# Sink rows of v by their own small transfers, and joint sink scores, in a windowed-attention kernel with a channel-mix FFN

## The chip, the cores and the metric

The kernel runs on one core of one Trainium2 chip. The metric is device time in microseconds for one execution, the median of several runs. A core has five engines that run side by side and wait for one another by semaphores: PE (matrix products), DVE (vector work), ACT (activations and copies), POOL (general work) and SP (which here issues transfers). SBUF is the on-chip memory, PSUM the eight banks into which PE writes.

## The reference

Attention with a window of 128 keys and 4 sink keys that every query sees, and on its output an FFN with a token shift:

```
q, k, v: (4, 8, 768, 64) float32      # batch, heads, positions, head width
scores = q @ k^T / sqrt(64)
keep   = (key position < 4) | (0 <= query position - key position < 128)
a      = softmax(where(keep, scores, -1e9));   attn = a @ v
x      = attn as (4, 768, 512);  x_prev = x shifted by one position
xk     = mu_k * x + (1 - mu_k) * x_prev;  xr = mu_r * x + (1 - mu_r) * x_prev
out    = sigmoid(xr @ w_r) * (relu(xk @ w_k)^2 @ w_v)      # 512 -> 1024 -> 512
```

## The kernel before

The work is cut into 12 units of 256 positions, three to each of the four sequences (u = 3b + T, with T = 0, 1, 2). A unit passes these steps, each a function that files its operations with a planner (`Plan.op`):

- `load` fetches q, k, v by transfers on SP's queue; two 1 MB halves of `w_k` and `w_v` and the whole of `w_r` come between the first units.
- `prepare` casts q and k to bf16 (`qb`, `kb`), transposes them on PE through a bank, or by a transposing transfer from a later unit on, and copies the bank to `qt` and `kt`; v is cast to `vb`, which has a column of ones beside each head's 64 values, so that a product gives the softmax sum as well.
- `attend` makes the scores of two head pairs at a time (`sc`), their exponentials on ACT (`e`), the mask as a product on DVE, and the products with the values (`o`, a bank for each head pair). DVE then takes the reciprocal of the sums (`rec`) and scales into `x`.
- `mix` transposes x into `xt` (on PE, or by transfers) and makes on DVE the difference to the previous position (`td`) and from it `xk` and `xr`.
- `ffn` does for the unit before: four groups of products with `w_k` (`kp` in the planner's keys, line L1139), relu (`rl`) on ACT and square (`kk`) on DVE, the gate's products (`rp`, L1170) with a tanh (`th`), and the products with `w_v` (`vp`, L1188 and, for the last block, L1108), which DVE joins with the gate into `ob` (L1197) for the store.

The sinks: in units with T = 1 or 2, the four sink keys lie outside the window for most queries. `sink_keys` places the four keys of each head from `kt` of the sequence's first unit into a small stationary matrix `ksink`. `sink_scores` (L835) makes for a unit the scores of all heads against the sinks, four products of 256 columns into one bank, and ACT makes their exponentials `es` (L842). For the values, once in each sequence, PE multiplies the whole first half of `vb` (128 rows of 512 columns) with a 0/1 matrix `spread` (L814), which puts the four sink rows of v onto the partitions where the sink scores of each head lie, and DVE multiplies the bank with a head mask `hmask` into `vsink` (L818, two buffers). `sink_values` (L924, or L909 in another tiling) adds the sinks' part to `o`.

Nothing is ordered at run time. `ORDER` lists for each engine the numbers of its operations, in the order in which it takes them, and `CHOICE` says for some operations which engine does them (or how PE is tiled). `Plan.schedule` walks these lists, hands out buffers and banks, and puts warm-up products on `warm` (L1251, L1254, L1248) where its own clock has PE waiting in the first 28 us. An engine waits at an operation until its inputs are there, and all that stands behind it in its list waits too. The numbers change whenever an operation is added or removed, so the two kernels' lists are not comparable by number; what follows therefore names operations by what they write.

Four pools matter around the change: two double banks for the scores, four single banks for everything else that PE writes, three buffers `ob`, and five `e`.

Of the kernel before, what the change touches and what calls it, by code (L numbers as in the profile page):

```python
# [8 lines left out]
FP32 = mybir.dt.float32  # L9
# [9 lines left out]
    80: "ACT", 81: "POOL", 82: "ACT", 83: "DVE", 84: "POOL", 85: "ACT", 86: "ACT",  # L19
    87: "ACT", 88: "ACT", 89: "DVE", 90: "DVE", 92: "ACT", 93: "ACT", 95: "ACT", 96:  # L20
    "POOL", 98: "ACT", 99: "DVE", 101: "DVE", 102: "POOL", 103: "ACT", 129: "POOL",
    131: "ACT", 132: "DVE", 134: "ACT", 135: "ACT", 137: "ACT", 138: "DVE", 140:
    "ACT", 141: "POOL", 142: "DVE", 144: "DVE", 151: "ACT", 160: "PE/tiles", 172:
    "PE/tiles", 183: "POOL", 185: "ACT", 186: "ACT", 188: "ACT", 189: "POOL", 191:
    "ACT", 192: "POOL", 194: "ACT", 195: "DVE", 196: "DVE", 198: "DVE", 205: "ACT",
    213: "ACT", 217: "ACT", 221: "ACT", 225: "ACT", 234: "SP", 238: "POOL", 242:
    "PE/full", 254: "PE/tiles", 265: "POOL", 267: "ACT", 268: "DVE", 270: "ACT",
    271: "POOL", 273: "DVE", 274: "DVE", 276: "ACT", 277: "POOL", 278: "ACT", 283:
    "DVE", 290: "DVE", 298: "ACT", 302: "ACT", 306: "ACT", 310: "ACT", 319: "SP",
    323: "SP", 346: "ACT", 348: "ACT", 349: "DVE", 351: "ACT", 352: "ACT", 354:  # L30
    "ACT", 355: "ACT", 357: "ACT", 358: "POOL", 359: "POOL", 361: "ACT", 368: "ACT",
    376: "ACT", 380: "ACT", 384: "ACT", 388: "ACT", 397: "SP", 401: "SP", 405:
    "PE/tiles", 417: "PE/tiles", 428: "POOL", 429: "POOL", 431: "ACT", 432: "POOL",
    434: "POOL", 436: "ACT", 437: "POOL", 438: "ACT", 440: "ACT", 447: "ACT", 455:
    "ACT", 459: "ACT", 463: "ACT", 467: "ACT", 476: "SP", 480: "SP", 484:
    "PE/tiles", 496: "PE/tiles", 507: "POOL", 508: "ACT", 510: "ACT", 511: "POOL",
    513: "ACT", 515: "ACT", 516: "ACT", 517: "ACT", 522: "ACT", 529: "ACT", 537:
# [38 lines left out]
TOGETHER = 2  # L76

OCT = range(1, 12)

WHOLE = (0,)  # L80

JOINT = ()

SWITCH = 95.0

LOADS = ("kq0", "v0", "kq1", "wka", "wkb", "v1", "wr", "wva", "wvb")
# [300 lines left out]
def kernel(  # L389
# [190 lines left out]
    def fill_later():  # L580
        for t in ksink + vsink:
            nc.vector.memset(t, 0.0)
# [729 lines left out]
```

## Time and profile before

| | |
|---|---|
| median of three runs | 163.79 us (162.93 to 163.96) |
| the profiled execution | 163.9 us, its span 162.2 us |
| busy PE, DVE, ACT, POOL | 152.7, 147.4, 119.9, 39.3 us |
| granted TensorE clock | 1.00 |
| moved by transfers | 35.16 MB |

In the profile, L12 means line 12 of the kernel, PEld is PE's weight load, and SPq or ACTq an engine's issuing of transfers. A name such as `kt` stands for all its buffers. A row of the chain or of the timeline begins with its start and length in us; in brackets stands how long the engine had been idle before it, and what released it. In the stretches, the columns behind the length are the busy time of PE, PEld, DVE, ACT and POOL with the instructions started, then the granted clock, the share of the transfer engines and GB/s. Busy time of PE overlaps from product to product, so 5 of 5 us does not mean that no product waited.

### The profile page before, as it was taken

The numbers are of one execution on the slowest core, as the hardware profiler recorded it, in microseconds if no ns is written. First come the engines' busy times: TensorE is split into PE (matmuls) and PEld (weight loads), VectorE is DVE, ScalarE is ACT, GpSimd is POOL, SyncE is SP. The second block draws the span as 40 slices with busy tenths as digits, with TensorE's granted clock in tenths as the row PEclk, the third lists the DMA queues.
The fourth block names the chain that finished last, engine by engine and source line by source line (L and its number), as shares of the span: only waits on it lengthen the run. The fifth ranks groups of instructions, "written<-read, shape, count | busy, mean of one in ns | idle before, by whom it ended". The sixth has DMA issues, their size and how long they took to land.

```text
span 162.2 us, 4697 instructions
## 1 busy us (share of the span) xinstructions
PE 152.7 (94%) x1857; PEld 99.4 (61%) x1857; DVE 147.4 (91%) x378; ACT 119.9 (74%) x194; POOL 39.3 (24%) x69
## 2 busy tenths in 40 slices
PE   7959779999999999999999999999999999999992
PEld 2545457964568567776566575865466865577541
DVE  6299989999999999999999999999999999998631
ACT  4699998999999899888689964878167985043420
POOL 6643330610662260242111006241010040001000
PEclk9999999999999999999999999999999999999999
DMA  4999999999988999999999999999999733351113
GB/s 140 251 353 249 391 342 295 368 401 312 211 265 215 259 233 156 237 266 144 223 213 211 303 220 207 196 265 164 265 168 206 168 89 103 65 195 68 65 65 129
DMA packets 78885, 35.16 MB, mean 217 GB/s; under 512 B 68744, under 2 KB 71056, under 8 KB 78864
## 3 DMA queue, kind: packets, MB, share of 16 engines
q1 hardware_dynamic: 78384, 33.63, 88.7%
q0 software_dynamic: 320, 1.05, 1.8%
q8 instruction: 14, 0.23, 0.7%
q10 hardware_dynamic: 160, 0.20, 0.3%
q14 instruction: 7, 0.06, 0.1%
HBM read 24.12 MB, written 6.29 MB: 188 GB/s over the span
## 4 chain that ended last, share of the span: by engine, by line
PE 75%; DVE 7%; SPq 5%; DMA 5%; ACT 3%; issue 2%; POOL 1%; DVEq 0%
PE bank L1188 24%; PE bank L1139 22%; PE bank L1170 12%; PE bank L971 6%; DMA ks<-in_k_dram 5%; PE sc L866 5%; SPq L483 2%; DVE e L952 2%; SPq L500 2%; ACT rl L1149 2%; PE bank L1012 2%; PE bank L754 1%; PE bank L924 1%; SPq L507 1%; DVE x L988 1%
## 5 line engine op out<-in xcount | busy, mean ns | idle before, releaser
L1139 PE MATMUL bank<-xk,wk_sb 128*128 128x256 bf16 x384 | 48.3, 273 | 0.0
L938 ACT ACTIVATE e<-sc 128x1024 bf16<-128x1024 f32 (+1 forms) x48 | 45.0, 965 | 2.3 <-PE sc L866 2.1
L1188 PE MATMUL bank<-wv_h,kk 128*128 128x512 bf16 x184 | 44.8, 379 | 0.0
L1139 PEld LDWEIGHTS <-wk_sb 128*128 128x128 bf16 x384 | 36.0, 98 | 7.2
L1149 ACT ACTIVATE rl<-bank 128x512 bf16<-128x512 f32 x47 | 27.2, 608 | 15.6 <-PE bank L1139 13.8
L952 DVE TENSOR_TENSOR e<-e,mask 128x1024 bf16<-128x1024 bf16 (+1 forms) x48 | 31.0, 659 | 0.0
L1188 PEld LDWEIGHTS <-kk 128*128 128x128 bf16 x184 | 17.0, 98 | 15.8
L1061 DVE SCALAR_TENSOR_TENSOR xr<-td,mu_all,xt 128x256 bf16<-128x256 bf16 x48 | 24.0, 514 | 0.0
L1170 PE MATMUL bank<-wr_sb,xr 128*128 128x512 bf16 x96 | 23.7, 379 | 0.4 <-DVE vsink L818 0.4
L1061 DVE SCALAR_TENSOR_TENSOR xk<-td,mu_all,xt 128x256 bf16<-128x256 bf16 x48 | 23.9, 526 | 0.1
L1161 DVE TENSOR_TENSOR kk<-rl 128x512 bf16<-128x512 bf16 x48 | 20.9, 451 | 1.8 <-ACT rl L1149 1.7
L1176 ACT ACTIVATE th<-bank 128x512 f32<-128x512 f32 x24 | 14.1, 598 | 10.9 <-PE bank L1170 10.9
L988 DVE TENSOR_TENSOR x<-bank,rec 128x256 bf16<-128x256 f32 x48 | 19.4, 416 | 0.3
L1197 DVE SCALAR_TENSOR_TENSOR ob<-th,bank 128x512 f32<-128x512 f32 x23 | 15.5, 679 | 2.7 <-ACT th L1176 2.5
L971 PE MATMUL bank<-vb,e 128*128 128x65 bf16 x352 | 16.4, 194 | 1.3 <-DVE e L952 1.2
L791 POOL CAST vb<-vs 128x512 bf16<-128x512 f32 x10 | 9.4, 948 | 31.8 <-DMA vs<-in_v_dram 22.1
L971 PEld LDWEIGHTS <-e 128*128 128x128 bf16 x352 | 13.8, 97 | 5.4 <-DVE e L952 2.5
L1170 PEld LDWEIGHTS <-xr 128*128 128x128 bf16 x96 | 8.8, 98 | 9.3 <-issue 0.5
L866 PEld LDWEIGHTS <-kt 64*64 64x64 bf16 (+1 forms) x496 | 8.9, 106 | 6.4 <-issue 3.8
L866 PE MATMUL sc<-qt,kt 64*64 64x128 bf16 (+4 forms) x496 | 12.6, 226 | 0.0
L1048 DVE TENSOR_TENSOR td<-xt 128x512 bf16<-128x512 bf16 x24 | 10.6, 455 | 0.0
L714 POOL CAST qb<-qs 128x512 bf16<-128x512 f32 x7 | 5.1, 722 | 21.8 <-DMA qs<-in_q_dram 21.8
(95 smaller groups left out, 150.9 us busy)
## 6 DMA issues: line engine op xcount, KB each, us to landing
vs<-in_v_dram SPq DMA_DIRECT2D x24, 256.0 KB, 5.0
out_dram<-ob SPq DMA_DIRECT2D x19, 256.0 KB, 3.9
ks<-in_k_dram SPq DMA_DIRECT2D x16, 256.0 KB, 5.1
qs<-in_q_dram SPq DMA_DIRECT2D x12, 256.0 KB, 4.0
qs<-in_q_dram SPq DMA_DIRECT2D x6, 512.0 KB, 5.8
ks<-in_k_dram SPq DMA_DIRECT2D x4, 512.0 KB, 8.4
w<-in_moe_w_k_dram SPq DMA_DIRECT2D x2, 1024.0 KB, 8.8
w<-in_moe_w_v_dram SPq DMA_DIRECT2D x2, 1024.0 KB, 10.4
```

The lines of the kernel that those rows point to most:

```text
L866: nc.tensor.matmul(out=sc[keys, a, o0 + f0 - q0:o0 + f1 - q0], lhsT=lhs[rows, keys], rhs=qs[rows, f0:f1], start=u not in BIAS, stop=True, ...
L938: nc.scalar.activation(out=buf[ek][:, :, lo:], in_=buf[sck][:, :, lo:], func=AF.Exp, scale=scale)
L952: nc.vector.tensor_tensor(out=at, in0=at, in1=m, op=ALU.mult)
L971: nc.tensor.matmul(out=o[:, g, a, :], lhsT=e[:, a, e0:e0 + 128], rhs=rhs, start=(T == 0 and i == 0), stop=(i == len(blocks) - 1), skip_gro ...
L988: P.op("DVE", dve(256), lambda ok=ok, rk=rk, c=c: nc.vector.tensor_tensor(out=buf["x", u][:, :, 128 * c:128 * c + 128].rearrange("p g (a d ...
L1061: nc.vector.scalar_tensor_tensor(out=buf[key][:, c, :], in0=buf[tk][:, i, :], scalar=mu[w][:, c:c + 1], in1=xt[:, c, t0 - 1:t0 + 255], op0 ...
L1139: nc.tensor.matmul(out=ps[:, i, :], lhsT=wk_sb[:, c, 128 * f:128 * f + 128], rhs=xk[:, c, :], start=(c == 0), stop=(c == NC - 1), skip_gro ...
L1149: nc.scalar.activation(out=buf[rk], in_=buf[psk].rearrange("p (i t) -> p i t", i=2), func=AF.Relu)
L1161: P.op("DVE", dve(512, 0.52), lambda f2=f2, rk=rk: nc.vector.tensor_tensor(out=buf["kk", u][:, 2 * f2:2 * f2 + 2, :], in0=buf[rk], in1=buf ...
L1170: nc.tensor.matmul(out=buf[psk], lhsT=buf["xr", u][:, c, 128 * g:128 * g + 128], rhs=wr_sb[:, c, :], start=(c == 0), stop=(c == NC - 1))
L1188: nc.tensor.matmul(out=buf[psk], rhs=wv_h[:, f, :], lhsT=buf["kk", u][:, f, 128 * g:128 * g + 128], start=(f == 0), stop=(f == NF - 1))
L1197: P.op("DVE", dve(512), lambda psk=psk, tk=tk, bk=bk: nc.vector.scalar_tensor_tensor(out=buf[bk], in0=buf[tk], scalar=1.0, in1=buf[psk], o ...
```

## The change

The sink rows of v no longer come from `vb` of each sequence's first unit. Four transfers on ACT's queue, of 32 rows of 64 floats each, fetch them for all sequences and heads at the start (`vs32`), an engine casts them (`vs16`, here DVE), four products of 64 columns with a wider `spread` (a matrix for each sequence) put them in one bank, ACT copies the bank to `rows` (with a column of ones), and DVE makes `vsink` for each sequence from `rows` and `hmask`, both bf16 in SBUF; `vsink` has four buffers now and is no longer cleared. `spread` is made by eight small copies on POOL in place of two, ahead of the mask of the first units; POOL's `make_sinks` goes. In sequences 1, 2 and 3 (`JOINT`) the sink scores of T = 1 and T = 2 are made together, eight products in one bank, with one exponential of 512 columns; `prepare` of the third unit is filed ahead of `attend` of the second. All of `ORDER` and `CHOICE` is new.

```diff
-JOINT = ()
+JOINT = (1, 2, 3)
...
 ORDER = {
     "PE": (
-        94, 91, 107, 78, 97, 100, 105, 118, 110, 115, 130, 136, 143, 133, 121, 139,
+        101, 81, 98, 112, 104, 77, 107, 123, 115, 120, 148, 141, 135, 126, 138, 144,
...
-    spread = tile1([128, 128], BF16, "spread")
+    spread = tile1([128, B, 128], BF16, "spread")
+    vs32 = tile1([128, D], FP32, "vs32")
+    vs16 = tile1([128, D], BF16, "vs16")
+    rows = tile1([128, B, D + 1], BF16, "rows")
...
-    vsink = [tile1([128, H, D + 1], BF16, f"vsink{i}") for i in range(2)]
+    vsink = [tile1([128, H, D + 1], BF16, f"vsink{i}") for i in range(B)]
...
-        for t, value in ((ones, 1.0), (spread, 0.0), (hmask, 1.0)):
+        for t, value in ((ones, 1.0), (spread, 0.0), (hmask, 1.0), (rows, 1.0)):
...
-        for t in ksink + vsink:
+        for t in ksink:
...
     def make_spread():
-
+        to = spread.rearrange("p b (k i w) -> p b i k w", k=2, i=2)
+        at = ident.rearrange("p (s b i k a) -> p a s b i k", s=NS, b=B, i=2, k=2)
         for a in range(2):
-            nc.gpsimd.tensor_copy(
-                out=spread[0:NS, :].rearrange("p (c w) -> p c w", w=32)[:, :, 4 * a:4 * a + NS],
-                in_=ident[0:NS, 0:NS].unsqueeze(1).to_broadcast([NS, NP, NS]))
+            for j in range(NS):
+                nc.gpsimd.tensor_copy(out=to[:, :, :, :, NS * a + j], in_=at[:, a, j])
...
-    def make_sinks():
-        for t in vsink:
-            nc.gpsimd.tensor_copy(out=t[:, :, D:D + 1], in_=hmask[:, :, D:D + 1])
...
+    def load_sinks():
+        for j in range(NS):
+            nc.scalar.dma_start(out=vs32[B * H * j:B * H * j + B * H, :],
+                                in_=v[:, :, j, :].rearrange("b h d -> (b h) d"))
+    P.op("ACT", 1200.0, load_sinks, -98, writes=["vs32"], service=90.0, descs=128, lag=2500.0)
...
+    def spread_sinks():
+        for b in range(B):
+            nc.tensor.matmul(out=buf["vsp"][:, D * b:D * b + D], lhsT=spread[:, b, :], rhs=vs16,
+                             start=True, stop=True)
+    P.op("PE", 150.0, spread_sinks, -38, take=[("bank", "vsp")], reads=["spread", "vs16"],
+        writes=["vsp"])
...
+    for b in range(B):
+        P.op("DVE", dve(520, 0.52), lambda b=b: nc.vector.tensor_tensor(
+            out=vsink[b], in0=rows[:, b, :].unsqueeze(1).to_broadcast([128, H, D + 1]),
+            in1=hmask, op=ALU.mult), 30 * b - 30, port=True, reads=["rows", "hmask"],
+            writes=[("vsink", b)])
...
-        psk = ("vsp", b)
-        P.op("PE", 220.0, lambda: nc.tensor.matmul(
-            out=buf[psk].rearrange("p (h d) -> p h d", h=H), lhsT=spread,
-            rhs=buf["vb", u][:, 0, :, 0:D], start=True, stop=True), rank + 4,
-            take=[("bank", psk)], hold=[("vb", u)], reads=["spread", ("vb", u, 0)], writes=[psk])
-        P.op("DVE", dve(512), lambda: nc.vector.tensor_tensor(
-            out=vsink[b % 2][:, :, 0:D], op=ALU.mult, in1=hmask[:, :, 0:D],
-            in0=buf[psk].rearrange("p (h d) -> p h d", h=H)), rank + 4, hold=[psk],
-            reads=[psk, "hmask", "sinks"], writes=[("vsink", b % 2)])
```

Three places of the new order. The first is PE's list at the very start, between the first transposes of unit 0's q and those of its k. Before (the product on `warm` is a warm-up):

```order
L759 MATMUL bank_63<-ident,qb_82 128x128
L1251 LDWEIGHTS warm
L1251 MATMUL bank_64<-warm 128x512
L759 LDWEIGHTS kb_79
L759 MATMUL bank_66<-ident,kb_79 128x128
```

And now, where `vs_151` is the cast rows of the sinks (this is the last of four such products):

```order
L675 LDWEIGHTS spread
L675 MATMUL bank_64<-vs_151,spread 128x64
L785 LDWEIGHTS kb_79
L785 MATMUL bank_66<-ident,kb_79 128x128
L785 LDWEIGHTS kb_79
```

The spreading of all sequences now stands ahead of the first transposes of k; before, the first sequence's stood behind the first scores, and the others' in the later units.

The second is DVE's list after the memsets of the start, up to the first mask (`e_94`). Before:

```order
L719 CAST kb_79<-ks_67 128x4x2x64
L719 CAST qb_82<-qs_70 128x4x2x64
L777 COPY qt_89<-bank_64 128x512
L660 COPY mu_all<-bank_63 128x8
L952 TENSOR_TENSOR e_94<-e_94,mask_147 128x2x384
```

And now:

```order
L745 CAST qb_82<-qs_70 128x4x2x64
L668 CAST vs_151<-vs_150 128x64
L803 COPY qt_89<-bank_63 128x512
L803 COPY kt_85<-bank_66 128x512
L745 CAST qb_82<-qs_70 128x4x2x64
L687 TENSOR_TENSOR vsink_157<-rows,hmask 128x520
L745 CAST kb_79<-ks_67 128x4x2x64
L803 COPY kt_85<-bank_64 128x512
L967 TENSOR_TENSOR e_94<-e_94,mask_147 128x2x384
```

The cast of the sinks' rows, both copies of unit 0's kt and the second sequence's vsink now stand on DVE ahead of the first mask; the copies of kt were ACT's.

The third is DVE's list near the end, from unit 11's last mask (`e_97`) to the last piece of unit 10's xk (`xk_115`), `x_109` being unit 11's. Before:

```order
L952 TENSOR_TENSOR e_97<-e_97,mask 128x1024
L985 RECIPROCAL rec_103<-bank_66 128x4
L988 TENSOR_TENSOR x_109<-bank_66,rec_103 128x2x128
L985 RECIPROCAL rec_106<-bank_63 128x4
L985 RECIPROCAL rec_105<-bank_65 128x4
L988 TENSOR_TENSOR x_109<-bank_65,rec_105 128x2x128
L1048 TENSOR_TENSOR td_110<-xt_156 128x512
L988 TENSOR_TENSOR x_109<-bank_63,rec_106 128x2x128
L1048 TENSOR_TENSOR td_112<-xt_156 128x512
L1061 SCALAR_TENSOR_TENSOR xk_115<-td_110,mu_all,xt_156 128x256 x2
L1061 SCALAR_TENSOR_TENSOR xk_115<-td_112,mu_all,xt_156 128x256 x2
```

And now, from the same mask, without its first rows on:

```order
L1076 SCALAR_TENSOR_TENSOR xk_115<-td_111,mu_all,xt_161 128x256
L1212 SCALAR_TENSOR_TENSOR ob_132<-th_129,bank_63 128x512
L1063 TENSOR_TENSOR td_110<-xt_161 128x512
L1000 RECIPROCAL rec_105<-bank_64 128x4
L1000 RECIPROCAL rec_106<-bank_65 128x4
L1076 SCALAR_TENSOR_TENSOR xk_115<-td_110,mu_all,xt_161 128x256
L1003 TENSOR_TENSOR x_109<-bank_64,rec_105 128x2x128
L1003 TENSOR_TENSOR x_109<-bank_65,rec_106 128x2x128
L1076 SCALAR_TENSOR_TENSOR xk_115<-td_110,mu_all,xt_161 128x256
L1076 SCALAR_TENSOR_TENSOR xk_115<-td_111,mu_all,xt_161 128x256
```

An `ob` has moved into the piece and the xk are spread among unit 11's x. On PE, between unit 11's last values and the first `kp` of unit 10, five half products with `w_v` stood before and three stand now.

More of the change, by code (lines that the diff above doesn't have):

```diff
@@ L18 @@
 CHOICE = {
[L19 to L37, printed above, removed]
-    "ACT", 541: "ACT", 545: "ACT", 549: "ACT", 558: "SP", 562: "SP", 585: "ACT",
@@ L52 @@
+    "ACT", 984: "SP", 988: "SP", 991: "ACT", 995: "ACT", 999: "ACT", 1003: "DVE",
+    1012: "SP",
 }
```

79 lines of the change are left out of this document (55 added, 24 removed), and 137 rows, old and new, of the table ORDER.

## Prediction

> **What bounds the kernel now.** I read first the page's lines on busy time and the chain that ended last, then that chain in order of time, then the engines' busy time by stretches, and last the single instructions at the places that those three point to.
>
> ```profile
> PE 152.7 (94%) x1857; PEld 99.4 (61%) x1857; DVE 147.4 (91%) x378; ACT 119.9 (74%) x194; POOL 39.3 (24%) x69
> PE 75%; DVE 7%; SPq 5%; DMA 5%; ACT 3%; issue 2%; POOL 1%; DVEq 0%
> ...
> 10.17 8.74 DMA ks<-in_k_dram
> 18.97 0.82 POOL kb L710
> ...
> 110.02 0.61 DVE vsink L818
> 110.67 1.02 PE bank L1170 x4
> ...
> 8.70:24.00 15.30, 11.60 (x219) 7.52 (x219) 14.39 (x38) 14.38 (x24) 5.39 (x9) 1.00 1.07 340
> 24.00:60.00 36.00, 35.61 (x477) 23.87 (x479) 35.93 (x91) 34.78 (x56) 11.97 (x16) 1.00 1.03 283
> 60.00:100.00 40.00, 40.00 (x524) 27.07 (x517) 39.43 (x101) 33.47 (x56) 9.26 (x13) 1.00 1.18 220
> 100.00:140.60 40.60, 40.23 (x500) 25.88 (x499) 39.85 (x105) 26.30 (x42) 6.34 (x10) 1.00 0.85 174
> ```
>
> The first two lines say PE. The chain in time (start and length in us) says where it does not hold: before about 24 us the chain runs over the keys of unit 2 (the transfer lands at 18.97) and what is made of them, and at 110 it runs over DVE. The stretches (length, then busy PE, weight loads, DVE, ACT, POOL) say something that the shares hide: from 8.7 to 140.6 us DVE is busy 129.6 of 131.9 us. PE and DVE are a dead heat, and PE takes its work in a fixed order, so whichever is later at a handover sets the pace. Two handovers show it:
>
> ```profile
> 20.70 0.42 DVE L1021 COPY xt<-bank 128x512 bf16<-128x512 bf16 x1 [0.65 <-PE bank L1012]
> 23.56 0.41 PE L971 MATMUL bank<-vb,e 128*128 128x65 bf16 x8 [0.87 <-DVE e L952]
> 23.82 1.03 PE L1139 MATMUL bank<-xk,wk_sb 128*128 128x256 bf16 x8
> ...
> 135.77 0.67 DVE L952 TENSOR_TENSOR e<-e,mask 128x1024 bf16<-128x1024 bf16 x1
> 137.06 4.48 PE L1188 MATMUL bank<-wv_h,kk 128*128 128x512 bf16 x20
> 138.89 1.67 DVE L1061 SCALAR_TENSOR_TENSOR xk<-td,mu_all,xt 128x256 bf16<-128x256 bf16 x4
> 141.38 2.78 PE L1139 MATMUL bank<-xk,wk_sb 128*128 128x256 bf16 x24
> ```
>
> The FFN begins at 23.82 behind a wait for a mask. At the end DVE finishes unit 10's xk at 140.56 (138.89 + 1.67) and PE wants it at 141.38: 0.8 us to spare after 130 us. From there on the chain is PE's alone, so the time is the start of that L1139 plus a fixed tail of 22.5 us (163.9 - 141.4).
>
> **The change, part by part.** All sums are against the profiled execution, 163.9 us with a span of 162.2; the median of the runs is 163.79, 0.1 below.
>
> *PE.* Four spreading products of 512 columns go, four of 64 columns come at the very start; three of the four stood in the full stretch. In sequences 1 to 3 two sink-score operations become one of twice the length.
>
> ```profile
> 47.19 0.22 PE bank L814
> 47.41 0.22 PE bank L835 x4
> 47.63 0.46 PE sc L866 x16
> ...
> 66.97 0.24 PE bank L924 x8
> 67.21 0.33 PE sc L866 x16
> ...
> PE bank L1170 <- DVE vsink L818: 0.4, 1, 0.4
> ```
>
> A spreading product holds PE 0.22 us: 3 x 0.22 = 0.66. Four sink-score products take 0.22, and the scores behind them take 0.13 more than behind products of their own tiling (0.46 against 0.33). Eight in one go cost between 0.22 and 0.44, so each joint operation saves 0 to 0.22; I take the middle, 3 x 0.11 = 0.33, and 0.13 for one change of tiling fewer in the new order. With the wait that ends at 110.67 (the last row: 0.4 us in which PE was held because DVE had not yet read a spreading product's bank), PE is relieved by 0.66 + 0.33 + 0.13 + 0.4 = 1.5 us, bounds 1.0 to 1.8.
>
> *DVE from the first mask to unit 10's xk.* I counted both orders between these two points. Masks, reciprocals, normalisations, xk, xr, kk and td are the same in number; the rest differs by: 4 vsink products fewer of the old kind and 3 new ones; 4 q casts and 2 v casts fewer; one ob, 2 xt copies, one wk cast, one wv cast, one k cast, one relu and one copy of mu more; a qt copy in the place of a kt copy.
>
> ```profile
> L818 DVE TENSOR_TENSOR vsink<-bank,hmask 128x512 bf16<-128x512 f32 x4 | 2.7, 681 | 0.0
> L952 DVE TENSOR_TENSOR e<-e,mask 128x1024 bf16<-128x1024 bf16 x32 | 21.7, 688 | 0.0
> L1197 DVE SCALAR_TENSOR_TENSOR ob<-th,bank 128x512 f32<-128x512 f32 x23 | 15.5, 679 | 2.7 <-ACT th L1176 2.5 <-PE bank L1188 0.2
> L710 DVE CAST qb<-qs 128x512 bf16<-128x512 f32 x5 | 1.9, 421 | 0.1
> L791 DVE CAST vb<-vs 128x512 bf16<-128x512 f32 x4 | 1.7, 419 | 0.0
> L1021 DVE COPY xt<-bank 128x512 bf16<-128x512 bf16 x4 | 1.7, 414 | 0.7 <-PE bank L1012 0.7
> L677 DVE CAST wk_sb<-w 128x1024 bf16<-128x1024 f32 x1 | 0.7, 689 | 0.0
> L675 DVE TENSOR_SCALAR wv_h<-w 128x1024 bf16<-128x1024 f32 x1 | 0.7, 684 | 0.0
> ```
>
> An instruction's successor starts about 0.08 before its end, so each counts 0.08 less than its mean: 0.60 for the long ones (the relu, which reads a bank of the same size as ob's, is put with them), 0.34 for the short. The new vsink product (520 elements, all operands bf16 in SBUF) has no row. Its ends are 0.34 (half of a 1024-element mask, with the fixed part) and 0.61 (as the old one on PSUM); I take 0.34, nearest to the mask, which also reads a repeated bf16 operand. Then: -4 x 0.60 + 3 x 0.34 - 6 x 0.34 + 0.60 + 2 x 0.33 + 3 x 0.60 + 0.34 + 0.1 = +0.1 us. **DVE is given nothing back in this stretch**: what vsink frees is spent on copies and casts taken over from ACT and POOL. With the other end it would be 0.9 us more.
>
> The row fits a rule of the Trainium skill, "Vector Engine (DVE) Microarchitecture Reference", section "5.1 Performance modes": a product of two tensors does two elements a cycle only where all operands are 2-byte and step by one. Its stricter reading asks for 4-byte alignment, which the 130-byte rows here would break (the 0.61 end, 0.8 us more in the sum); the page reports that alignment made no difference, and rows of odd length neither. No run here shows an odd row yet.
>
> *The start.* Here the change costs. PE now has the spreading ahead of the first transposes of k, and it waits for the spread matrix (POOL) and for four small transfers issued by ACT and a cast of them on DVE.
>
> ```profile
> 0.81 0.56 ACTq L551 DMA_DIRECT2D ob<-in_moe_mu_r_dram  x1
> 1.47 0.26 ACTq L551 DMA_DIRECT2D ob<-in_moe_mu_k_dram  x1
> 4.42 0.18 POOL L603 CAST ident<-ident 8x8 f32<-8x8 bf16 x1
> 5.99 0.59 ACT L777 COPY kt<-bank 128x512 bf16<-128x512 bf16 x1
> 6.00 0.32 POOL L630 COPY spread<-ident 4x16 bf16<-4x16 bf16 x2
> 6.63 0.51 PE L866 MATMUL sc<-qt,kt 64*128 64x256 bf16 x8
> ...
> vs<-in_v_dram SPq DMA_DIRECT2D x24, 256.0 KB, 5.0
> out_dram<-ob SPq DMA_DIRECT2D x1, 64.0 KB, 2.0
> ```
>
> Two small copies took 0.32, so eight take 1.3; begun at 4.60 they end at 5.9. The transfers are issued behind one of mu, at 0.26 to 0.56 each: the last leaves at 2.7 to 3.9. The nearest rows for landing are 2.0 us (the smallest with a time) and 5.0 (a load in the same traffic), so they land between 4.7 and 8.9. I take the lower part, 4.7 to 5.8, since 8 KB is nearest to the 64 KB row; then spread is the later one. Spreading ends at 6.2, four transposes of k take until 6.6, the copy of kt, on DVE now, until 7.3 (0.59 on ACT, by DVE's other reads of a bank up to 0.69), scores at about 7.4 in place of 6.63: **0.8 us late**, bounds 0.3 and 3.3. ACT and DVE have little idle time behind that point to make it up (14.38 and 14.39 of 15.30 us in the first stretch), so DVE's first mask moves from 8.7, where that stretch begins, to 9.5.
>
> The Trainium skill, "DMA: Bandwidth & Descriptors", section "Rules for kernel authors", speaks against this edit: below 64 KB a transfer is mostly overhead. In its section "Anatomy of one DMA" the fixed part is about 2.0 us for transfers that GpSimd issues; by that estimate the last would land at 4.7 to 5.9, spread would still be later, and the sum would not change. It lowers the chance of the late case below.
>
> *What the start gains.*
>
> ```profile
> DVE rec L985 <- PE bank L971: 0.8, 3, 0.4
> ```
>
> In the new order the first FFN product does not stand behind DVE's copy of unit 1's xt, which made DVE wait 0.65 and PE 0.87. DVE thereby has its wait of 0.65 back, and of its three waits for PE's values (0.8 in all, the row above) I let half go, 0.4, as PE is earlier. The keys of unit 2 keep their place in the queue of loads and land at 19 as before; the FFN then starts at about 23.2, 0.6 earlier.
>
> *Other engines.* ACT has five sink exponentials for eight, and fewer casts and copies; it is busy 74%, so that is hidden. Four stores move from POOL's queue to SP's, behind loads already issued; nothing waits for a store but a buffer of three.
>
> *The sum.* DVE reaches unit 10's xk at 140.56 + 0.8 + 0.1 - 0.65 - 0.4 = 140.4. In the new order PE has only three half products (2.6 us) in place of five between unit 11's last values and unit 10's FFN, so it stands waiting there: L1139 starts at 140.5 in place of 141.4. The tail holds the same products. 163.9 - 0.9 = 163.0, on the runs' scale **162.8 us**.
>
> **The rivals.**
>
> *PE sets the pace.* If DVE is quicker than counted (less held up by POOL, a start only 0.3 late), PE's relief comes through whole: 1.5 + 0.6 from the earlier start = 2.1, that is 161.8. For it: the chain is 75% PE; ACT and DVE need not share so many handovers early. Against: the sum of DVE's work. It decides where DVE ends xk before 139.3.
>
> *The sinks' rows land late.* PE's queue is in order: while it waits for the spreading, k isn't transposed, no score is made, and ACT and DVE stand still. With a landing at 8.9, cast and spreading end at 9.4 in place of 6.2, scores at 10.6; the start is 4.0 late, 3.2 more than forecast. All of it passes to DVE's finish: 163.0 + 3.2 = 166.2; with a landing at 7.5, 164.8. It becomes slower than before from a landing of about 6.8. For it: the first units' loads move at the same time, and such loads take 5.0. Against: 2.0 us for the smallest row.
>
> *The gain is eaten.* New waits between 24 and 60 us, where three engines are full at once (35.61, 35.93 and 34.78 of 36.0), or unit 10's handover later than counted, bring it back to 163.8.
>
> **How the numbers follow.** DVE's pace 0.42 (162.2 to 163.4), PE's pace 0.30 (161 to 162.1), eaten 0.14, rows late 0.14. About 1% is what a measurement of this kernel can tell from no change, so faster means below 162.15 and slower above 165.4. All of PE's pace and a sixth of the forecast lie below: 0.37. Of the late case two thirds lie above: 0.09. The rest is 0.54. The range of 8 in 10 leaves out the lowest tenth, under 161.2, and the worse part of the late case: 161.2 to 165.0.
>
> **What would show it.** The first scores start at 7.4 and not 6.6; a wait of PE for spread, or for the cast of the rows, stands ahead of them. The new vsink product lasts 0.4 us, not 0.68. No spreading product after 10 us, and a joint sink-score group of eight in 0.33. The first L1139 at 23.2. DVE busy over 97% to 140 us, and PE idle ahead of unit 10's L1139 behind DVE's xk. Wrong would be: PE never waiting there (PE's pace), scores after 8.5 us (rows late), or DVE with idle time of several us.

## The result, and the profile after

The changed kernel takes 169.47 us (median; 169.33 to 170.75), the kernel before 163.49 in the same comparison: a ratio of 1.0385 (it is worked out from all runs and not from the two medians), 95% interval 1.0322 to 1.0448. It is 3.9% slower, where 162.8 us and a range up to 165.0 were forecast. The profiled execution took 169.39 us, its span 167.7 (before: 163.9 and 162.2). Here and below a ratio leaves out executions more than 1.5% above the fastest of their kernel, which in sinks_first are four of twelve (166.1 to 166.6 us).

The timeline of ACT's queue, DVE and PE at the start of the changed kernel (start and length in us, engine, line, operation, and in brackets the idle time ahead of it and what ended it):

```profile
1.11 0.55 ACTq L551 DMA_DIRECT2D ob<-in_moe_mu_k_dram  x1
1.70 0.79 ACTq L664 DMA_DIRECT2D vs<-in_v_dram  x2
3.84 1.31 ACTq L664 DMA_DIRECT2D vs<-in_v_dram  x2
6.29 0.27 ACTq L551 DMA_DIRECT2D ob<-in_moe_mu_r_dram  x1
...
4.83 0.58 PE L785 MATMUL bank<-ident,qb 128*128 128x128 bf16 x4 [0.35 <-POOL ident L597]
4.98 1.16 POOL L635 COPY spread<-ident 128x16 bf16<-128x16 bf16 x8
5.21 1.17 PE L1269 MATMUL bank<-warm 128*128 128x256 f32 x2
6.60 0.62 ACT L745 CAST kb<-ks 128x512 bf16<-128x512 f32 x1 [4.30 <-DMA qs<-in_q_dram]
8.85 0.46 DVE L668 CAST vs<-vs 128x64 bf16<-128x64 f32 x1 [4.58 <-DMA vs<-in_v_dram]
9.36 0.37 PE L675 MATMUL bank<-vs,spread 128*128 128x64 bf16 x4 [2.98 <-DVE vs L668]
9.54 0.61 PE L785 MATMUL bank<-ident,kb 128*128 128x128 bf16 x4
9.95 1.17 PE L1269 MATMUL bank<-warm 128*128 128x256 f32 x2
11.48 0.82 PE L881 MATMUL sc<-qt,kt 64*128 64x256 bf16 x8
```

and two rows of PE in the kernel before:

```profile
5.55 0.40 PE L759 MATMUL bank<-ident,kb 128*128 128x128 bf16 x4
5.79 0.65 PE L1254 MATMUL bank<-warm 128*128 128x256 f32 x2
```

Three things are to be seen. The third and fourth of the sinks' transfers are issued only from 3.84 on, and ACT's queue is occupied until 6.56, so ACT casts its first half of k at 6.60. The rows land at 8.85; DVE has been idle for 4.58 us by then, and PE for 2.98 when the cast is done. And what PE does behind that wait is slow: four transposes take 0.61, a pair of fp32 warm-up products 1.17 and eight scores 0.82, where in the kernel before the same rows read 0.40, 0.65 and 0.51. The rows of 4.83 and 5.21, ahead of the wait, are slow as well (0.58 and 1.17): in this execution PE had not become fast before the wait began. The first scores start at 11.48 instead of 6.63.

From the first FFN product to the end the two kernels take the same time. The first row below is the first FFN product (23.82 before), the second unit 10's (141.38 before):

```profile
29.15 1.48 PE L1154 MATMUL bank<-xk,wk_sb 128*128 128x256 bf16 x12
...
146.99 3.66 PE L1154 MATMUL bank<-xk,wk_sb 128*128 128x256 bf16 x32
```

From the one to the other are 117.84 us, 117.56 before; from unit 10's to the span's end 20.7, 20.8 before. So 5.3 of the span's 5.5 us are lost ahead of the first FFN product. The parts of the change that stand in the middle do what they should. A group of DVE's instructions (busy us, mean ns of one):

```profile
L687 DVE TENSOR_TENSOR vsink<-rows,hmask 128x520 bf16<-128x520 bf16 x4 | 1.7, 426 | 0.0
```

a piece of the chain in order of time:

```profile
61.20 0.33 PE bank L850 x8
```

and two stretches, before and, behind the dots, in the changed kernel (length, then busy PE, weight loads, DVE, ACT, POOL, clock, DMA share, GB/s):

```profile
40.00:60.00 20.00, 20.00 (x270) 12.48 (x272) 19.97 (x49) 19.29 (x33) 8.44 (x13) 1.00 1.00 230
60.00:80.00 20.00, 20.00 (x268) 14.22 (x264) 19.46 (x50) 17.01 (x30) 5.35 (x9) 1.00 1.23 212
...
40.00:60.00 20.00, 19.32 (x241) 12.07 (x240) 19.58 (x47) 18.66 (x30) 9.98 (x11) 1.00 0.77 188
60.00:80.00 20.00, 19.18 (x293) 12.96 (x292) 19.78 (x50) 16.44 (x28) 7.23 (x11) 1.00 1.21 221
```

A vsink product takes 0.43 us and a joint group of sink scores 0.33. But in the stretches PE is now idle for 0.7 and 0.8 us of 20, where it was busy throughout. From the first FFN product to unit 10's it is busy for 115.7 us instead of 116.8, in a stretch that is no shorter: the work taken off it became waiting.

### The profile page after: what moved, and what is told of

The parts are those of the page before. It is cut to its first block, busy times and chain, and to the rows that moved or that the text cites. A ratio compares the mean times of both kernels' runs of the same rounds, so it can differ in the third digit from the quotient of the medians.

```text
span 167.7 us, 4713 instructions
## 1 busy us (share of the span) xinstructions
PE 155.3 (93%) x1862; PEld 101.3 (60%) x1862; DVE 148.4 (89%) x381; ACT 118.4 (71%) x188; POOL 38.6 (23%) x70
## 4 chain that ended last, share of the span: by engine, by line
PE 72%; DVE 12%; issue 5%; ACT 4%; DMA 3%; SPq 1%; POOL 1%; DVEq 0%; POOLq 0%
PE bank L1154 23%; PE bank L1203 21%; PE bank L1185 12%; PE bank L986 6%; PE sc L881 5%; DMA vs<-in_v_dram 3%; DVE xk L1076 3%; DVE e L967 2%; ACT e L953 2%; PE bank L780 1%; PE bank L1027 1%; DVE x L1003 1%; SPq L507 1%; DVE td L1063 1%; DVE kk L1176 1%
## 5 line engine op out<-in xcount | busy, mean ns | idle before, releaser
L953 ACT ACTIVATE e<-sc 128x1024 bf16<-128x1024 f32 (+1 forms) x48 | 44.4, 961 | 6.7 <-PE sc L881 6.6
L967 DVE TENSOR_TENSOR e<-e,mask 128x1024 bf16<-128x1024 bf16 (+1 forms) x48 | 31.7, 678 | 0.5 <-ACT e L953 0.5
L1076 DVE SCALAR_TENSOR_TENSOR xr<-td,mu_all,xt 128x256 bf16<-128x256 bf16 x48 | 22.4, 484 | 0.0
L986 PE MATMUL bank<-vb,e 128*128 128x65 bf16 x352 | 15.7, 194 | 0.4 <-DVE e L967 0.2
L881 PE MATMUL sc<-qt,kt 64*64 64x128 bf16 (+4 forms) x496 | 13.1, 228 | 0.7 <-ACT kt L798 0.4
L1063 DVE TENSOR_TENSOR td<-xt 128x512 bf16<-128x512 bf16 x24 | 10.6, 457 | 0.0
L740 POOL CAST kb<-ks 128x512 bf16<-128x512 f32 x6 | 4.5, 761 | 20.9 <-DMA ks<-in_k_dram 20.8
```

The source lines that it names most:

```text
L881: nc.tensor.matmul(out=sc[keys, a, o0 + f0 - q0:o0 + f1 - q0], lhsT=lhs[rows, keys], rhs=qs[rows, f0:f1], start=u not in BIAS, stop=True, ...
L953: nc.scalar.activation(out=buf[ek][:, :, lo:], in_=buf[sck][:, :, lo:], func=AF.Exp, scale=scale)
L967: nc.vector.tensor_tensor(out=at, in0=at, in1=m, op=ALU.mult)
L986: nc.tensor.matmul(out=o[:, g, a, :], lhsT=e[:, a, e0:e0 + 128], rhs=rhs, start=(T == 0 and i == 0), stop=(i == len(blocks) - 1), skip_gro ...
L1076: nc.vector.scalar_tensor_tensor(out=buf[key][:, c, :], in0=buf[tk][:, i, :], scalar=mu[w][:, c:c + 1], in1=xt[:, c, t0 - 1:t0 + 255], op0 ...
```

## Experiments

The table gives, from each profiled run, the start of the first scores, of the first FFN product (A) and of unit 10's (B) in us, and the ratio to the kernel before with its 95% interval. The times in us are of one execution and the ratio is of all, and the two need not agree: the profiled execution was far the fastest of one_transfer (164.8 us, the others 166.5 and more) and the fastest of late_one (164.7, median 166.1), and the slowest of before_gate (170.7, the others 168.7 to 169.0) and of rows_between (166.2, median 165.6).

| kernel | scores | A | B - A | ratio |
|---|---|---|---|---|
| before | 6.63 | 23.82 | 117.56 | 1 |
| changed | 11.48 | 29.15 | 117.84 | 1.0385 [1.0322, 1.0448] |
| no_transfers | 7.54 | 23.36 | 117.95 | 0.9984 [0.9949, 1.0019] |
| spread_late | 8.74 | 26.17 | 118.31 | 1.0159 [1.0100, 1.0218] |
| one_transfer | 8.21 | 24.25 | 117.88 | 1.0118 [1.0040, 1.0197] |
| late_one | 6.92 | 24.44 | 117.60 | 1.0093 [1.0046, 1.0140] |
| before_gate | 10.96 | 28.58 | 119.32 | 1.0317 [1.0255, 1.0379] |
| kept_warm | 10.32 | 26.83 | 118.51 | 1.0213 [1.0162, 1.0264] |
| two_transfers | 10.42 | 27.09 | 117.93 | 1.0170 [1.0105, 1.0235] |
| rows_between | 6.77 | 25.30 | 118.21 | 1.0052 [1.0018, 1.0086] |
| sinks_first | 7.09 | 23.48 | 118.25 | 1.0019 [0.9986, 1.0052] |
| dve_relief | 6.96 | 25.39 | 118.49 | 1.0087 [1.0046, 1.0127] |
| less_pe | 7.88 | 24.38 | 117.52 | 0.9978 [0.9930, 1.0026] |
| short_masks | 7.82 | 24.04 | 117.22 | 0.9955 [0.9915, 0.9995] |
| less_both | 7.64 | 23.51 | 117.33 | 0.9930 [0.9880, 0.9979] |
| less_stores | 7.52 | 23.50 | 117.61 | 0.9987 [0.9950, 1.0025] |
| less_all | 7.58 | 23.84 | 115.45 | 0.9872 [0.9805, 0.9938] |

### The start

**no_transfers**: the changed kernel without the four transfers.

```diff
-        for t, value in ((ones, 1.0), (spread, 0.0), (hmask, 1.0), (rows, 1.0)):
+        for t, value in ((ones, 1.0), (vs32, 0.0), (spread, 0.0), (hmask, 1.0), (rows, 1.0)):
...
-        for j in range(NS):
-            nc.scalar.dma_start(out=vs32[B * H * j:B * H * j + B * H, :],
-                                in_=v[:, :, j, :].rearrange("b h d -> (b h) d"))
+        pass
```

> The changed kernel without the four transfers of the sinks' rows (their tile is cleared by a memset instead, so the sinks' values are left out); every order is as in the changed kernel. Theory A, the rows' landing at 8.8 us holds PE, and the delay passes to the end: PE then waits for spread alone, the first scores start at about 7.4 in place of 11.5, and the time falls by about 4.1, to 164.5 to 165.5. Theory B, the new order loses the time in later stretches: within 1 us of 169.4. Theory C, ACT's issuing (until 6.6 us) holds the first cast of k, and that alone counts: as A here, since the issues are gone too.

The whole loss is gone (5.3 us, where Theory A had 4.1); the casts, the spreading and the new orders are all still there. PE's spreading then waits for 0.3 us only, by the row for DVE's copy of qt (it ends at 6.19, the spread matrix at 6.18):

```profile
6.24 0.29 PE L673 MATMUL bank<-vs,spread 128*128 128x64 bf16 x4 [0.29 <-DVE qt L801]
7.54 0.50 PE L879 MATMUL sc<-qt,kt 64*128 64x256 bf16 x8
```

**spread_late** leaves the four transfers and moves what waits for them (cast, spreading, vsink) behind unit 0's first values. **one_transfer** has one transfer of 128 rows in place of the four, in the same orders. **late_one** has both, with the transfer behind those of mu. (Below, PE's list is that of spread_late and late_one, the transfer that of one_transfer and late_one.)

```diff
-        101, 81, 98, 112, 104, 77, 107, 123, 115, 120, 148,     # PE's list (81 the spreading)
+        101, 98, 112, 104, 77, 107, 123, 115, 120, 81, 148,
...
+        nc.scalar.dma_start(out=vs32, in_=v[:, :, 0:NS, :].rearrange("b h j d -> j (b h) d"))
```

> The changed kernel with the same four transfers, but the spreading on PE behind unit 0's first values, the cast of the rows and two vsink products on DVE behind the first two masks, and the copy to rows on ACT behind the third exponential. Theory A: the wait is gone from PE's list; scores at about 8.4, since ACT still issues until 6.6 and only then casts k (6.6 to 7.2, transposes 7.6, copy 8.3): 3.1 earlier, about 166.3. If ACT's issuing doesn't matter, scores at 6.6 and 164.5. Theory B: within 1 us of 169.4.

> The changed kernel with one transfer of 128 rows in place of four of 32, same place in ACT's queue and same orders. If the issues on ACT's queue are what is late (two of the four left only at 3.8 to 5.2 us): the transfer leaves at about 2.3, lands at 5 to 6, spread is the later one, scores at 7.4 to 7.8, time 165 to 165.7. If a small transfer takes its 3.7 us in this traffic whatever it is issued behind, it lands at about 6 and the result is nearly the same, 165.5; if it queues behind the loads of q and k, it lands at 8 to 9 and the time stays at 169. Theory B: 169.

> Both edits: one transfer, issued behind both of mu, and the spreading behind unit 0's first values. Theory A with C: ACT casts k at about 4.6, transposes until 5.4, scores at 6.4 to 6.8, as before the change, 4.8 earlier than in the changed kernel: 164.5 if all else stays, and 163.0 if the remaining terms of the prediction's sum (no wait of DVE at 20 us, PE relieved) hold as well. Theory B: 168 to 169.

In spread_late nobody waits for the rows, yet the FFN begins 2.8 us later than without transfers. ACT's queue still stands, and ACT's cast of k with it (its timeline):

```profile
1.69 0.79 ACTq L656 DMA_DIRECT2D vs<-in_v_dram  x2
3.87 1.27 ACTq L656 DMA_DIRECT2D vs<-in_v_dram  x2
6.59 0.26 ACTq L543 DMA_DIRECT2D ob<-in_moe_mu_r_dram  x1
6.89 0.62 ACT L737 CAST kb<-ks 128x512 bf16<-128x512 f32 x1 [4.59 <-DMA qs<-in_q_dram]
```

late_one differs from it only in the transfers: there ACT casts k at about 4.7, and the FFN begins 1.7 us earlier. That is the price of the standing queue; the other 1.1 of the 2.8 us are there in late_one too, with its moved pieces.

In one_transfer's timeline nothing stands, and the rows land at 5.95; 0.9 us is left in this execution, where the ratio over all says 1.2%:

```profile
1.70 0.65 ACTq L663 DMA_DIRECT2D vs<-in_v_dram  x1
2.39 0.52 ACTq L551 DMA_DIRECT2D ob<-in_moe_mu_r_dram  x1
4.64 0.62 ACT L743 CAST kb<-ks 128x512 bf16<-128x512 f32 x1 [2.33 <-DMA ks<-in_k_dram]
5.95 0.92 DVE L666 CAST vs<-vs 128x64 bf16<-128x64 f32 x1 [1.69 <-DMA vs<-in_v_dram]
```

late_one has its scores at 6.92, nearly as early as before, and still no earlier FFN, so its median of 166.1 us missed both forecast times. That the moved pieces delay masks and copies of the first units is likely; no run shows it by itself.

**before_gate**: the kernel before with its own orders, and only the gate.

```diff
+        for j in range(NS):          # behind ACT's table load
+            nc.scalar.dma_start(out=vs32[B * H * j:B * H * j + B * H, :],
+                                in_=v[:, :, j, :].rearrange("b h d -> (b h) d"))
...
+                if (u, name, half) == (0, "k", 0):
+                    nc.vector.tensor_copy(out=vs16, in_=vs32)
+                    nc.tensor.matmul(out=buf[psk][:, 256:320], lhsT=ident, rhs=vs16,
+                                     start=True, stop=True)
```

> The kernel before with its own orders, and of the change only the gate at the start: the four transfers of the sinks' rows behind ACT's table load, their cast on DVE, and a dummy product of 64 columns on PE that waits for the cast ahead of unit 0's k transposes. Joint scores, spreading products, vsink products and the new orders are all left out. Theory (the start carries the whole loss): first scores at about 11 to 11.5 us as in the changed kernel, the first FFN product 4.5 to 5.5 us later than in the kernel before, time 168 to 169.5 us where the kernel before has 163.5 (ratio 1.028 to 1.037). Rival (the new orders in the middle share the loss): the gate is taken up in part by slack behind the start, ratio 1.01 to 1.02.

The gate alone makes the old kernel 3.2% slower, against 3.9% for the whole change, and the intervals overlap: the new orders have little to do with it. Its stretches also show what the slow products were (the last three columns: granted clock, DMA share, GB/s):

```profile
5.00:8.00 3.00, 0.61 (x5) 0.34 (x6) 0.38 (x1) 1.20 (x2) 1.93 (x8) 1.00 0.86 210
9.00:18.00 9.00, 8.64 (x64) 5.44 (x64) 4.90 (x14) 6.11 (x10) 2.49 (x5) 0.50 1.05 308
19.00:23.00 4.00, 3.57 (x80) 1.99 (x78) 3.97 (x10) 4.00 (x8) 1.73 (x2) 1.00 1.07 395
```

After an idle stretch of 2.6 us PE was granted half its clock for 10 us, from 8.1 to 18.4. The other three executions read a mean clock of 1.00. In the changed kernel's trace the clock column stays at 1.00 there, so the lengths are all that tells: 0.82 for the scores in both. (Its three other executions have a mean clock of 0.98 to 0.99.)

**kept_warm**: the changed kernel, with PE busy while it waits.

```diff
     def spread_sinks():
+        for i in range(12):
+            nc.tensor.matmul(out=buf["vsp"], lhsT=warm[:, 0:128], start=True, stop=True,
+                             rhs=warm.unsqueeze(1).to_broadcast([128, 2, 256]))
```

> The changed kernel, with twelve extra products of 512 columns on PE while it waits for the sinks' rows (their results are overwritten). In the changed kernel, the transposes, the fp32 warm-up products and the first scores behind the wait of 3 us lasted 0.61, 1.17 and 0.82 us where they last 0.40, 0.65 and 0.51 in the kernel before. Theory (PE runs slowly after a long idle stretch, whatever it waited for): with PE kept busy they are back at 0.40, 0.65 and 0.51, the first scores come at 10.4 to 10.9 instead of 11.5, and the time is 0.5 to 1.0 us below the changed kernel's (ratio to the kernel before 1.030 to 1.036). Rival (they are slow because their inputs come late or because of the transfers that run then): durations and the first scores as in the changed kernel, ratio 1.037 to 1.040.

```profile
5.57 2.75 PE L675 MATMUL bank<-warm 128*128 128x512 bf16 x12
9.15 0.39 PE L788 MATMUL bank<-ident,kb 128*128 128x128 bf16 x4
9.37 0.65 PE L1272 MATMUL bank<-warm 128*128 128x256 f32 x2
10.32 0.50 PE L884 MATMUL sc<-qt,kt 64*128 64x256 bf16 x8
```

The lengths are back, and the FFN begins 2.3 us earlier, more than the theory's 0.5 to 1.0: useless products win 1.7% (1.0213 against 1.0385). The mean granted clock of its four executions is 1.00. Of the 5.8 us between no_transfers and the changed kernel at that point, 2.3 are PE's clock and 3.5 the late rows together with ACT's standing queue. One thing is not the same: here the transposes at 4.86 already took 0.38, ahead of the extra products, so the two executions differ by more than the edit. That a wait alone takes a fast PE's clock is shown by two_transfers, below.

**two_transfers** has two transfers of 64 rows; **rows_between** has one transfer behind mu and the waiting work between the first scores and the first masks; **sinks_first** puts one transfer ahead of mu, and on POOL the identity and the spread matrix ahead of the masks.

```diff
+        for j in range(0, NS, 2):     # two_transfers
+            nc.scalar.dma_start(out=vs32[B * H * j:B * H * j + 2 * B * H, :],
+                                in_=v[:, :, j:j + 2, :].rearrange("b h j d -> j (b h) d"))
...
-        69, 67, 79, 68, 97, 82,       # sinks_first: ACT's list (79 the sinks' transfer)
+        69, 79, 67, 68, 97, 82,
-        76, 75, 72, 74, 73,           # POOL's (72 ident, 74 spread)
+        72, 74, 76, 75, 73,
```

> The changed kernel with the sinks' rows in two transfers of 64 rows instead of four of 32. Open is why ACT's queue stood still behind two of the four, from 2.49 to 3.84 us. Theory (behind mu_k's transfer and two more the queue stands still until about 3.84 us, and goes on from there): the two transfers go out at 1.70 to 2.6 as before, now with all rows in them, and mu_r's waits until 3.84 or later; the rows land at 5.9 to 6.5, the first scores come at 8.2 to 8.7, ratio to the kernel before 1.010 to 1.020. Rival (the stand comes from the number of rows asked for, not of transfers): the second transfer goes out only at 3.8, rows land at 8 or later, first scores at 10.5 or later, ratio above 1.025.

> The changed kernel with one transfer of 128 rows instead of four, issued behind both transfers of mu, and the work that waits for it moved behind unit 0's first scores: cast on DVE behind the second q cast, spreading on PE behind the scores, rows on ACT behind the first two exponentials, the two vsink products behind the first masks. Theory (the loss is the landing, and the four issues on ACT, and nothing else): rows land at 5.5 to 6.5 us and nobody waits for them, the first scores come at 6.9, the first FFN product at 23.3 to 23.8, and the time is 163.0 to 163.8 us, ratio 0.994 to 1.000. Rival (the pieces cost as much wherever they stand between the first scores and the first FFN product, as in the run that put them later): first FFN product at 24.2 to 24.5, ratio 1.004 to 1.010.

> The changed kernel, with the sinks' rows in one transfer ahead of both transfers of mu on ACT's queue, and on POOL the identity and the spreading matrix ahead of both masks. Theory (the loss is the late rows, and PE's half clock that follows the wait for them): issued at 0.81 instead of 1.70, the rows land at 4.8 to 5.2, the spreading matrix is ready by 3.6, nothing waits for either, PE keeps its full clock, first scores at 6.6 to 7.2, first FFN product at 22.9 to 23.6, ratio to the kernel before 0.992 to 0.999. Rival (the spreading costs the start what it did without transfers, or mu comes late instead): first scores at 7.5 or later or a wait for mu, ratio 1.000 to 1.006.

The timeline of two_transfers:

```profile
1.71 0.64 ACTq L664 DMA_DIRECT2D vs<-in_v_dram  x1
2.38 0.51 ACTq L664 DMA_DIRECT2D vs<-in_v_dram  x1
3.85 0.26 ACTq L551 DMA_DIRECT2D ob<-in_moe_mu_r_dram  x1
5.06 0.65 PE L1269 MATMUL bank<-warm 128*128 128x256 f32 x2
8.05 0.20 DVE L668 CAST vs<-vs 128x64 bf16<-128x64 f32 x1 [3.77 <-DMA vs<-in_v_dram]
8.30 0.37 PE L675 MATMUL bank<-vs,spread 128*128 128x64 bf16 x4 [2.59 <-DVE vs L668]
8.90 1.16 PE L1269 MATMUL bank<-warm 128*128 128x256 f32 x2
```

and of sinks_first:

```profile
1.11 1.15 ACTq L655 DMA_DIRECT2D vs<-in_v_dram  x1
4.40 0.37 DVE L658 CAST vs<-vs 128x64 bf16<-128x64 f32 x1
5.50 0.28 PE L665 MATMUL bank<-vs,spread 128*128 128x64 bf16 x4
```

In two_transfers the queue stands still behind its third transfer, as in the changed kernel: the theory's half that counts transfers holds. But the rows land at 8.05 and not by 6.5, though the last was asked for by 2.89; that half fell, and that the ratio of 1.0170 lies in the theory's range is luck. PE's rows show what a wait does: the same pair of products took 0.65 us ahead of an idle stretch of 2.59 us and 1.16 behind it, and the granted clock is 0.50 from 8.0 to 11.4.

The landings in order: asked for from 1.11 to 2.26 us (sinks_first), the rows are there by 4.40; from 1.70 to 2.35 (one_transfer), at 5.95; the last from 2.38 to 2.89 (two_transfers), at 8.05; by 4.23 (before_gate), at 8.41; by 5.15 (the changed kernel), at 8.85. Which place the rows get among the 256 KB loads that SP asks for from 0.81 on fits this; it was not tested by itself. sinks_first waits for nothing there, and its scores (7.09) and FFN (23.48) come as the theory had it, but it is no faster than the kernel before (its ratio is the rival's): the best that a version of the whole change gave. rows_between missed its forecast, and its ratio is the rival's. Nobody waited long for its rows, but in the profiled execution PE, busy for 2.0 of the 3.4 us up to 10.8, fell to half its clock all the same:

```profile
11.00:16.00 5.00, 4.41 (x40) 3.23 (x38) 3.76 (x12) 3.94 (x8) 1.84 (x3) 0.50 1.12 298
18.00:23.00 5.00, 4.67 (x79) 2.73 (x76) 4.76 (x11) 4.99 (x9) 2.06 (x3) 1.00 1.09 352
```

Whether that is why it missed is open: five of its twelve executions have a mean clock of 1.00 and took 164.9 to 165.8 us.

### The middle: where PE's relief went

**dve_relief** is rows_between with three pieces taken off DVE (choices 809 and 810 from DVE to POOL, 521 to ACT).

> The kernel of the run rows_between with three pieces taken off DVE behind the first FFN product: unit 10's two casts of v on POOL (0.43 us each on DVE) and one copy of xt of unit 5 on ACT (0.41), together 1.27 us of DVE's work, whose sum with the rest stays the same. Theory (DVE paces the middle in the changed orders, so PE's relief of 1.5 us became PE's waits): unit 10's first FFN product comes 0.8 to 1.3 us earlier against the first FFN product than in rows_between, ratio to the kernel before 0.986 to 0.992. Rival (PE paces after all, or the two give back to one another at once): less than 0.4 us earlier, ratio within 0.002 of that of rows_between.

It is no sooner: 1.27 us less of DVE's work bought nothing, which speaks against the prediction's "DVE's pace" (the work went to POOL and ACT, though, and was not left out). The next five start from no_transfers and leave out work, each of one engine, or of several. (A first run for the shorter masks, less_dve, left them whole; it repeats no_transfers, with B - A of 118.5 and a ratio of 1.0026 [0.9988, 1.0064].)

```diff
-                    for c in range(NC):                                          # less_pe
+                    for c in range(NC - (2 <= u <= 8 and f < 4)):
...
-            def masked(ek=ek):                                                   # short_masks
+            def masked(ek=ek, part=T > 0 and 4 <= u <= 8 and k < 2):
...
+                if part:
+                    at, m = at[:, :, 0:64], m[:, :, 0:64]
...
-                return lambda: queue.dma_start(out=out[b, s0:s0 + 128, :], in_=buf[bk])   # less_stores
+                n = 64 if 1 <= u <= 8 else 128
+                return lambda: queue.dma_start(out=out[b, s0:s0 + n, :], in_=buf[bk][0:n])
```

> The kernel without transfers (rows cleared, the sinks' values left out), and of 28 of PE's FFN products in units 2 to 8 one of their four parts left out: 28 times 0.11, or 3.1 us less of PE's work behind the first FFN product. Theory (DVE paces the middle): unit 10's first FFN product comes less than 1 us sooner behind the first one than in the kernel without transfers (117.95 us there). Rival (PE paces it): 2.3 to 3.1 us sooner.

> The kernel without transfers (rows cleared, the sinks' values left out), and of eight of DVE's mask products in units 4, 5, 7 and 8 only a quarter of the columns, so that masking is left out there too: eight times about 0.4, or 3.2 us less of DVE's work behind the first FFN product. Theory (DVE paces the middle): unit 10's first FFN product comes 2.3 to 3.2 us sooner behind the first one than the 117.95 us of the kernel without transfers. Rival one (DVE and PE hand the pace to one another): 0.3 to 1.5 us sooner. Rival two (the DMA engines, busy for 98% of that stretch, set it): within 0.3 us.

> Both cuts together: the eight short mask products on DVE (3.2 us less) and the 28 left-out parts of PE's FFN products (3.1 us less), in the kernel without transfers. Theory (DVE paces the middle): as with the short masks alone, 2.3 to 3.2 us sooner than 117.95. Rival one (they hand the pace to one another): 2.3 to 3.2 us sooner here, where each cut alone gave under 1.5. Rival two (the DMA engines set it): within 0.5 us here too.

> The kernel without transfers (rows cleared, the sinks' values left out), with the 16 stores of the outputs of units 1 to 8 cut to 64 of their 128 rows, the other rows left unwritten: 16 times 128 KB less for the DMA engines, or 5.4 us at the 385 GB/s that the window from 26 to 33 us moved. PE's and DVE's work are whole. Theory (the DMA engines, at 99% of the stretch from 23 to 141 us, set it): unit 10's first FFN product comes 1.5 to 2.6 us sooner behind the first one than the 117.95 us of the kernel without transfers, and then DVE's 115.3 us of work stop it. Rival (the engines' waits for one another set it, and transfers only lie waiting in queues): within 0.5 us.

> The short stores together with the short masks (3.2 us less on DVE) and the 28 left-out parts of PE's FFN products (3.1 us less), which without the short stores brought 0.6 us. Theory (the DMA engines set the stretch): 3 to 5.4 us sooner than 117.95. Rival (the engines' waits for one another set it): under 1.2 us sooner, as without the short stores.

Against 117.95, less work on PE brought B - A 0.43 us, on DVE 0.73, on both 0.62, on the DMA engines 0.34; on all three 2.50 us. Since no_transfers and its repeat lie 0.6 apart, only the last is clearly more than nothing. The queue of loads, stores and transposes in the stretch from 23 to 141 us, as a share of 16 engines, in no_transfers:

```profile
q1 hardware_dynamic: 67270, 26.02, 99.2%
```

and in less_all:

```profile
q1 hardware_dynamic: 67104, 24.41, 93.2%
```

In that stretch of 118 us, no_transfers has PE busy for 114.8, DVE for 115.3 and the DMA engines 99%. Each of the expectations that named one engine as the pace fell, DMA's too. The reading that fits is that the three are level: about 3 us taken from PE, from DVE or from both stay with the DMA engines, and 5.4 us of transfers with PE and DVE. It is not fully shown. It rests on one execution of each kernel, the ratios of less_both and less_all (0.9930 and 0.9872) have intervals that overlap, and the share of the DMA engines is the time that packets took (it reads 1.23 and 1.21 in stretches above), so that 99% need not mean that they could move no more: from 26 to 33 us no_transfers moved 387 GB/s, over the whole stretch 223. PE with the DMA engines, and DVE with them, were not tried.

## Why the prediction was wrong

- **The landing (the step that failed).** "I take the lower part, 4.7 to 5.8, since 8 KB is nearest to the 64 KB row": the row was picked by size. It landed 2.0 us after its issue, but as a store at the end, where transfers take 29% of the DMA engines' time (the last 7.2 us) and two stores of 256 KB took 2.0 us as well: size was not what made it short. These transfers stood among the first loads (89% from 0.8 to 9 us), and the row of 5.0 in the same traffic was the nearer one. Measured: 8.85, where the sum had 5.8 at most.
- **The issue.** "0.26 to 0.56 each: the last leaves at 2.7 to 3.9" multiplied a price of one. The last ended at 5.15, because the queue stood from 2.49 to 3.84. That ACT's own cast of k stands behind its issues was not in the sum; by spread_late against late_one it costs 1.7 us where nobody waits for rows.
- **A rival, and its price.** "The sinks' rows land late" is what happened, at its upper end: landing 8.9 was to give scores at 10.6 and 166.2 us. That its landing was met is luck: the last transfer was asked for by 5.15 and not 3.9, and took 3.7 us from there and not 5.0. With a landing of 8.85 the scores came at 11.48, the time at 169.5. Missing was the clock: the rival let PE stand still for 3 us and go on at full speed. By kept_warm that is 2.3 us. The remaining 1.0 is the gain that the sum counted on and that did not come: without the transfers the profiled execution takes 164.0 us, where the sum has 163.0. The Trainium skill, "TensorE: Matmul & The Clock Gate", section "Part 1: The HAM clock gate", says that after an idle window of about 3.4 us PE gets half its clock until it has been busy for about as long. The runs agree on the half (0.50), and in two_transfers on the time that it lasts (3.4 us). In rows_between the half clock lasted 6.8 us and in before_gate 10.2, two and three times as long; and an idle stretch of 2.6 us was enough to lose the clock in two_transfers and before_gate, while rows_between lost it without such a stretch, with PE busy for 2.0 of 3.4 us.
- **The fixed part that was weighed.** From the Trainium skill, "DMA: Bandwidth & Descriptors", section "Anatomy of one DMA", the prediction took a fixed part of about 2.0 us as an estimate and with it lowered the late case's chance. From the end of the issue the rows took at most 2.1 us in sinks_first, but 3.6, 5.2 and 3.7 in one_transfer, two_transfers and the changed kernel: measured, a small transfer in this traffic is not priced by a fixed part.
- **Right.** The spread matrix (1.16 us, ready at 6.14; 1.3 and 5.9 forecast), the vsink product (0.43, by the nearest row 0.34 to 0.61), the joint group (0.33), and with the transfers gone scores at 7.54 (7.4 forecast) and the FFN at 23.36 (23.2, for which the prediction shows no sum). The loss at the start passed through whole, as the rival said.
- **Half right.** PE and DVE were read as a dead heat, and PE's relief as worth only what DVE lets through. The DMA engines were missing from it; in the same stretch of the kernel before their queue reads 98.8%, too. If the three are level, the gain of 0.9 us was not to be had. Without transfers the kernel is as fast as before and not faster, as the rival "The gain is eaten" has it.
- **Small slips.** 163.0 less 0.1 is 162.9 and not 162.8, and the other end of the vsink product is 0.8 us more by the sum's own terms, not 0.9. Neither changes the outcome.

## What to carry to other kernels

Price a transfer at the start by the loads it stands among, and by its place in their order as far as the runs here go, not by its size; and count what its engine's own work loses behind the issues. Where PE must wait some 3 us, add what its clock costs afterwards, or keep it busy with products that nobody needs. Before counting a gain in a stretch that two engines fill, look at the DMA engines' share too: where three are that busy, relief of one or two was worth a fraction of itself here.

## What was not expected of the hardware

- ACT's queue took three transfers (mu and two of the sinks') and stood until 3.84 or 3.85 us in the changed kernel and in two_transfers, whether 32 or 64 rows each; in before_gate a fourth waited until 3.91 behind mu and three. In each the first load of q is there at that very time (in the changed kernel DVE begins to cast it at 3.84). What the queue waits for is open.
- PE fell to a granted clock of 0.50 without one long wait: in rows_between from 10.8 us, behind 3.4 us in which it was busy for 2.0; dve_relief's execution did the same (2.0 of 3.4 us up to 10.9). In late_one 2.3 of 3.4 us, from 11.0 to 14.4, did not cost the clock.
- The stretches at half clock lasted 3.4 us (two_transfers), 6.8 (rows_between, dve_relief) and 10.2 (before_gate): in these traces the clock changed only at multiples of about 3.4 us.
